# A chunked linear-attention recurrence and a two-layer MLP: the attention's instructions put in one planned order, the triangular inverse on blocks of 16, PSUM emptied by ScalarE in two places

## The chip, the cores and the metric

The kernel runs on one core of one Trainium2 chip. The metric is the device time of one execution in microseconds (us). Three runs of the kernel before took 845.59, 844.03 and 843.01 us; their median is 844.03 us.

## The reference

Six inputs of shape 4 x 8 x 768 x 40 (batch, heads, time, width) go through a recurrence with a 40 x 40 state per batch and head. The result, 3072 tokens of 320 values, goes through an MLP of 320 -> 2048 -> 320. The weights arrive in double precision.

```python
for t in range(S):
    y[:, :, t] = einsum('bhd,bhde->bhe', rt, state)
    Sa = einsum('bhde,bhe->bhd', state, at)
    state_decay = state * wt[:, :, None, :] - einsum('bhd,bhe->bhde', Sa, bt)
    state = state_decay + einsum('bhd,bhe->bhde', vt, kt)
...
h = x @ w_in
g = h * tanh(softplus(h))
return g @ w_out
```

## The kernel before

**Chunks.** The 768 time steps are cut into 12 chunks of 64. The 32 pairs of batch and head lie on two halves of the partitions (al), two groups (be) and eight slots. Inside a chunk the recurrence is turned into matrix products; between chunks only the state is carried. All attention work is fp32, where one matmul leaves two records in the profile (a transpose one).

**Preparation** (`pre_a`, once for each chunk and each be, 24 in all) loads decays and inputs (wa, bk), runs a forward and a backward scan over the decays on VectorE (lines 147, 157), scales a, b and k with them (152, 170), and has ScalarE copy the scaled a into ad (155). TensorE multiplies ad with bk (186, tile pa); ScalarE and VectorE take the results out of PSUM into GP (188, 189), HA (190) and, masked, HA (191). TensorE transposes bk (202) and ScalarE copies it to bkn (203). The backward scan writes into the place where a lay, so it waits for ScalarE's copy of a.

**Inverse** (`pre_inv` and `post_inv`, once for two chunks, six in all): 128 triangular 32 x 32 matrices lie across the partitions as lanes. VectorE transposes them in (209), then eliminates 30 rows one after another, each with a product into tmp (214) and an addition into XL (216), and transposes them out (218, 220). TensorE joins two 32-blocks to a 64-block with 32-wide products (232, 241); ScalarE lays the pieces out in bdT (249 to 251); TensorE forms the key products from bdT and HA (258), and ScalarE copies them to KT (260).

**Step** (`step_a` to `step_c`, once for each chunk, 12 in all, for two groups g): ScalarE copies the state ST into VS (277); TensorE multiplies VS with KT (284, tile pu); ScalarE negates the result into UVT (286). Then come products with r (314, tile pq, masked by VectorE into UVQ in 316), transposes of UVT (293) and of the state (304), and the products for the output y and the new state (334, 339). VectorE adds the new state from PSUM (342) and scales it (346); ScalarE copies y (343). GpSimd's queue stores y and the scan P to DRAM and loads the next chunk's r and v. "Double step" below means two chunks: one inverse, four preparations, two steps.

**MLP.** `load_x` reads y and P of a chunk back, multiplies them (565) and splits the product into a high and a low part (566 to 568). `mlp1` makes four first-layer groups (583, tile ph), `mlp2` the second layer (603 to 605, tile po), three groups later. The weights are turned from double precision into a high and a low single-precision part by `split`: a DMA into cv_d, then ScalarE (459), three VectorE operations (461 to 463), ScalarE (494) and VectorE (495). One such job covers 512 columns of w_in or 640 of w_out. Three jobs run early, nine for w_in late in the attention (`first`), three for w_out behind them (`second`), five in the MLP (`third`). They use one buffer each up to the MLP, and `first` may start only once all preparations have given back their memory.

**What sets the order.** The scheduler of the tile layer orders each engine's instructions. It is steered by priorities: a table OFF of offsets for each kind of work, ORDER and SORD for the sequence in which the source names it. It works on single instructions, so matmuls of two pieces of work may alternate on TensorE.

## Time and profile before

| | |
|---|---|
| median of three runs | 844.03 us |
| profiled execution, first to last instruction (the only time that its page gives) | 843.5 us |
| instructions in the profile | 18796 |
| TensorE matmul busy / VectorE / ScalarE / GpSimd | 89% / 55% / 51% / 12% |
| chain that ended last, by engine | PE 62%, DVE 15%, ACT 15%, issue 5%, DMA 2% |
| HBM traffic | 48.79 MB read, 11.86 MB written, 72 GB/s over the span |

PE is TensorE's matmuls, PEld its weight loads, DVE VectorE, ACT ScalarE, POOL GpSimd, SP the engine that issues most DMAs. Busy times of matmuls include a modelled end, so neighbouring matmuls overlap in the listing: the rate of a block is read from the start of its first matmul to the start of the next block. PEclk is the clock granted to TensorE, as a share of full speed. A share over the whole span mixes the attention with the MLP, which keep different engines busy.

### The profile page before, as it was taken

To read this page: it belongs to the slowest core of one execution; us is meant where nothing else is said; L and a number is where in the kernel's file an instruction comes from. 1 tells how busy PE (TensorE), PEld (TensorE's weight loads), DVE (VectorE), ACT (ScalarE), POOL (GpSimd) and SP (SyncE) were. 2 spreads that over 40 slices of the span, in tenths; PEclk is the share of its full clock that TensorE was granted. 3 is DMA by queue.
4 is the path that set the end of the run, shared out by engine and by line. 5 is a ranking of instruction groups with operands and counts; after the bars stand their busy time and mean duration, and the time that the engine had idled before them with its cause. 6 is when DMAs were issued, how large, how long until landed. Compare 5 with 4: busy or idle time off the path is not lost.

```text
span 843.5 us, 18796 instructions
## 1 busy us (share of the span) xinstructions
PE 748.6 (89%) x7816; PEld 695.6 (82%) x7816; DVE 462.0 (55%) x975; ACT 429.0 (51%) x937; POOL 103.3 (12%) x182
## 2 busy tenths in 40 slices
PE   2645898998989889889799899999999999999998
PEld 2534697887868778778768799999999999999998
DVE  6789879739899658788924639221222222122110
ACT  4533647774586866566738546333333333333331
POOL 8100012113122023221101200000000000000000
PEclk9855689899999999899959999999999999999999
DMA  6422223323423233323425734211120111100000
GB/s 177 134 71 64 74 63 73 90 67 105 129 81 80 66 88 103 82 67 96 123 66 142 179 109 128 54 35 36 38 54 25 31 54 35 35 21 16 16 1 32
DMA packets 58212, 61.91 MB, mean 73 GB/s; under 512 B 25536, under 2 KB 48704, under 8 KB 58128
## 3 DMA queue, kind: packets, MB, share of 16 engines
q1 hardware_dynamic: 49296, 40.94, 17.6%
q0 software_dynamic: 8832, 19.79, 9.5%
q8 instruction: 61, 1.00, 0.5%
q14 instruction: 23, 0.19, 0.1%
HBM read 48.79 MB, written 11.86 MB: 72 GB/s over the span
## 4 chain that ended last, share of the span: by engine, by line
PE 62%; DVE 15%; ACT 15%; issue 5%; DMA 2%; ACTq 0%; DVEq 0%; SPq 0%
PE ph L583 21%; PE po L604 7%; PE po L605 7%; PE po L603 7%; PE pa L186 5%; PE pa L258 4%; PE pq L314 3%; PE pq L334 2%; DVE XL L216 2%; DVE tmp L214 2%; ACT ad L155 2%; PE pu L284 1%; DMA cv_d<-in_wo 1%; DVE P L147 1%; ACT bdT L250 1%
## 5 line engine op out<-in xcount | busy, mean ns | idle before, releaser
L583 PE MATMUL ph<-xh,w_ih 128*128 128x256 f32 x576 | 148.3, 283 | 0.5 <-ACT xh L566 0.5
L585 ACT ACTIVATE g<-ph 128x512 f32<-128x512 f32 x96 | 57.3, 598 | 179.3 <-PE ph L583 179.2
L589 DVE TENSOR_TENSOR gl<-g,gh 128x1024 fp32r<-128x1024 f32 x48 | 58.7, 1225 | 160.7 <-ACT gh L588 160.4
L583 PE MATMUL ph<-xh,w_il 128*128 128x256 f32 x576 | 123.6, 283 | 0.0
L186 PE MATMUL pa<-bk,ad 128*128 128x168 f32 x384 | 85.0, 373 | 42.7 <-DVE bk L170 15.0
L604 PE MATMUL po<-w_ol,gh 128*128 128x320 f32 x384 | 118.8, 310 | 0.1
L605 PE MATMUL po<-w_oh,gl 128*128 128x320 f32 x384 | 118.4, 309 | 0.0
L603 PE MATMUL po<-w_oh,gh 128*128 128x320 f32 x384 | 117.7, 309 | 0.0
L186 PEld LDWEIGHTS pa<-bk,ad 128*128 128x128 f32 x384 | 70.8, 233 | 47.8 <-issue 22.8
L583 PEld LDWEIGHTS ph<-xh,w_ih 128*128 128x128 f32 x576 | 109.3, 190 | 0.7 <-ACT xh L566 0.7
L583 PE MATMUL ph<-xl,w_ih 128*128 128x256 f32 x384 | 101.2, 285 | 0.0
L583 PEld LDWEIGHTS ph<-xh,w_il 128*128 128x128 f32 x576 | 96.3, 190 | 0.0
L583 PEld LDWEIGHTS ph<-xl,w_ih 128*128 128x128 f32 x384 | 73.1, 190 | 0.8 <-issue 0.5
L604 PEld LDWEIGHTS po<-w_ol,gh 128*128 128x128 f32 x384 | 72.1, 188 | 0.5 <-DVE w_ol L495 0.5
L605 PEld LDWEIGHTS po<-w_oh,gl 128*128 128x128 f32 x384 | 72.1, 188 | 0.1
L603 PEld LDWEIGHTS po<-w_oh,gh 128*128 128x128 f32 x384 | 71.8, 188 | 0.0
L258 PE MATMUL pa<-bdT,HA 128*104 128x128 f32 x384 | 57.0, 304 | 9.0 <-ACT bdT L251 7.3
L258 PEld LDWEIGHTS pa<-bdT,HA 128*104 128x104 f32 x384 | 49.9, 190 | 14.4 <-ACT bdT L251 9.1
L216 DVE TENSOR_TENSOR XL<-XL,tmp 128x30 f32<-128x30 f32 (+9 forms) x180 | 59.0, 328 | 2.4
L214 DVE TENSOR_TENSOR tmp<-XL 128x30 f32<-128x30 f32 (+9 forms) x180 | 58.5, 325 | 2.5
L314 PE MATMUL pq<-bdr,UVT 128*128 128x128 f32 x384 | 57.3, 294 | 2.3 <-DVE UVQ L316 1.5
L314 PEld LDWEIGHTS pq<-bdr,UVT 128*128 128x128 f32 x384 | 50.8, 205 | 4.0 <-DVE UVQ L316 1.9
(89 smaller groups left out, 1243.5 us busy)
## 6 DMA issues: line engine op xcount, KB each, us to landing
wa<-in_wa SPq DMA_DIRECT2D x48, 162.5 KB
bk<-in_bk SPq DMA_DIRECT2D x48, 160.0 KB
cv_d<-in_wi SPq DMA_DIRECT2D x12, 512.0 KB
cv_d<-in_wo SPq DMA_DIRECT2D x8, 640.0 KB
pD<-P POOLq DMA_DIRECT2D x48, 81.2 KB, 2.2
VS<-in_vN POOLq DMA_DIRECT2D x24, 160.0 KB, 3.6
UVT<-in_vD POOLq DMA_DIRECT2D x24, 160.0 KB, 3.9
bdr<-in_rD POOLq DMA_DIRECT2D x24, 160.0 KB, 4.4
```

Of the source, the lines that this page charges most:

```text
L155: A.copy(ad[q, :, :, al], a[q].rearrange("p (s k t) -> p s k t", k=2, t=32))
L186: PE.matmul(pt[:, j], ad[:, s0 + j].rearrange("p k a t -> p (k a t)"), bk[:, s0 + j], start=(j == 0), stop=True, skip_group_check=True)
L214: V.tensor_tensor(out=tv, in0=X[:, i + 1:32, i:i + 1].broadcast_to([128, 31 - i, i]), in1=X[:, i:i + 1, 0:i].broadcast_to([128, 31 - i, i] ...
L216: V.tensor_tensor(out=X[:, i + 1:32, 0:i], in0=X[:, i + 1:32, 0:i], in1=tv, op=ALU.add)
L258: PE.matmul(pk[:, j], ha[:, s0 + j], bd[:, s0 + j].rearrange("p a t -> p (a t)"), start=(j == 0), stop=True, skip_group_check=True)
L314: PE.matmul(pq[:, s], UVT[:, g * 4 + s, be * 128:be * 128 + 128], br[:, be, g * 4 + s].rearrange("p a t -> p (a t)"), start=(s == 0), stop ...
L583: PE.matmul(o, w, x, start=(j == 0 and n == 0), stop=(n == 7), skip_group_check=True)
L585: A.activation(g[:, f0:f0 + 2], ph, AF.Mish)
L589: V.tensor_tensor(out=gl, in0=g, in1=gh.bitcast(F32), op=ALU.subtract)
L603: PE.matmul(po[k], gh[:, j, t], oh, start=(f == 0), stop=False, skip_group_check=True)
L604: PE.matmul(po[k], gh[:, j, t], ol, start=False, stop=False, skip_group_check=True)
L605: PE.matmul(po[k], gl[:, j, t], oh, start=False, stop=(f == 15), skip_group_check=True)
```

## The change

**One order for the attention.** All attention work and the conversions up to the MLP are recorded as operations in a small planner (`Plan`): engine, a cost in us written in the source, what is read and written, which buffers are used. `order` then runs a list: it takes the engine that can start earliest, and on it, of the operations that can start within 0.05 us of that, the one with the longest chain of costs behind it; a change of tile shape on TensorE counts 0.13 us, the scaling of the state has 15 us added to its chain. The operations are issued in the order of their planned starts, and this order stands as it is. An operation on TensorE is a whole block of matmuls. The MLP proper is still ordered by the tile layer, behind it. OFF, ORDER and SORD go.

**The inverse** eliminates rows inside 16 x 16 blocks only, both diagonal blocks in one instruction (14 pairs of row updates for 30). The block below the diagonal comes from two further products on TensorE, 128 matmuls of 32 x 32 x 16 each (lines 357 and 362 of the new kernel), with a ScalarE copy between them and a VectorE addition behind them. There is one more transpose, of half the size, into TD.

**PSUM.** In preparation ScalarE copies all of HA (104 columns for 40), and VectorE masks it afterwards in SBUF, once for eight slots. For y, ScalarE copies the new state's part out of PSUM too (524), and VectorE adds once for eight slots (528). To make HA one piece, k and b change places in the input layout.

**Buffers.** The backward scan has a tile E of its own. Two tiles of four PSUM banks each serve the attention, stn and the late conversions have two buffers, r and bdT one. `first` converts six jobs of w_in, `second` the last three of w_in and three of w_out; `second` starts only when `first` has finished.

```diff
-SORD = 'a0 b0 u0 d0 a1 b1 u1 d1 c0 c1'
-
-
-def at(tc, k):
-    return tc.high_priority(offset=OFF[k]) if OFF.get(k) else nullcontext()
...
+    def order(self):
+        for o in reversed(self.ops):
+            o.tail = o.cost + o.lat + max((p.tail for p in o.post), default=0.0) + o.late
...
+            e = min(low, key=low.get)
+            best = max((o for o in ready if o.eng == e and start[o] <= low[e] + self.look), key=lambda o: (o.tail, -o.i))
...
+        out.sort(key=lambda o: o.start)
+        return out
...
-        for i in range(1, 31):
-            tmp = iw.tile([128, 240], F32, name="tmp", bufs=NTMP)
-            tv = tmp[:, 0:(31 - i) * i].rearrange("p (t j) -> p t j", j=i)
...
+        op('V', 0.2, lambda: V.memset(X[:, 16:32, 0:16], 0.0), w=['X'])
+        x = X[:, 0:1, 0:1]
+        for i in range(1, 15):
+            m = 15 - i
...
+        op('V', 1.0, lambda: V.transpose(TD[:, :, 0:16].rearrange("p u j -> p j u"), X[:, :, 0:16].rearrange("p t j -> p j t")), r=['X'], w=['TD'])
...
+        def m1():
+            for u in range(32):
+                for q in (slice(k * 32, k * 32 + 32) for k in range(4)):
+                    PE.matmul(zv(b1)[q, u], gp.t[q, u, 1], TT[q, u, 16:32], start=(u == 0), stop=True, skip_group_check=True)
...
+                    PE.matmul(zv(b2)[q, u], TD[q, u], X1[q, u], start=(u == 0), stop=True, skip_group_check=True)
+        op('P', 3.0, m1, r=['TT'] + allg, w=[b1], mode=32)
+        op('A', 0.54, lambda: A.copy(X1, zv(b1)), r=[b1], w=['X'])
+        op('P', 3.0, m2, r=['TD', 'X'], w=[b2], mode=32)
+        op('V', 0.62, lambda: V.tensor_tensor(out=TT[:, :, 16:32], in0=TT[:, :, 16:32], in1=zv(b2), op=ALU.add), r=[b2], w=['TT'])
...
-            A.copy(ha[:, s0:s0 + m, oa:oa + 40], pt[:, 0:m, 128:168])
-            V.tensor_tensor(out=ha[:, s0:s0 + m, oh:oh + 64], in0=pt[:, 0:m, ok:ok + 64],
-                            in1=maskH.unsqueeze(1).broadcast_to([128, m, 64]), op=ALU.mult)
+            op('A', 0.38, lambda s0=s0, m=m, pv=pv: A.copy(ha.t[:, s0:s0 + m], pv()[:, 0:m, o2:o2 + 104]), r=[b], w=[(ha, s0)])
...
-                V.tensor_tensor(out=stn[:, 2 * s0:2 * s0 + 4], in0=st[:, 2 * s0:2 * s0 + 4, 0:40], in1=py[:, :, 64:104], op=ALU.add)
+                op('A', 0.25, lambda s0=s0, pv=pv: A.copy(stn.t[:, 2 * s0:2 * s0 + 4], pv()[:, :, 64:104]), r=[b], w=[(stn, s0)])
...
+            op('V', 0.42, lambda: V.tensor_tensor(out=stn.t, in0=stn.t, in1=st[:, :, 0:40], op=ALU.add), r=[('ST', g)], w=[(stn, 0), (stn, 2)])
...
+    M.first(S, S.after(preps, lambda: (pctx.close(), M.open_first(S))))
+    M.second(S, S.after(preps + invs + S.ops[-1:], lambda: (ictx.close(), M.open_second(S))))
+    with tc.manual_schedule():
+        S.issue()
```

Where the instructions stand now is shown at three places. Names are output<-inputs; the last column is the shape, x32 a count.

First TensorE, where an inverse's 32-wide products (232, 241) meet the products of a step's output (334), late in the program before:

```order
L232 MATMUL pa<-TT,GP 32x32 x32
L314 MATMUL pq<-bdr_121,UVT 128x128 x5
L241 MATMUL pa<-X_4875,GP 32x32 x20
L334 MATMUL pq<-UVQ_119,bkn 64x104
L241 MATMUL pa<-X_4875,GP 32x32
L334 MATMUL pq<-UVQ_120,bkn 64x104
```

The last rows go on alternating, one matmul of each. TensorE at an inverse of the new kernel, behind the output products of the step before (519 ends them; 289 is a small product of preparation, 357 and 362 the two new blocks, 474 the state's transposes, 327 transposes of preparation, 379 the former 232):

```order
L519 MATMUL pl_161<-bdr,smd_141 64x2x64 x4
L289 MATMUL pr_162<-w_98,cst 64x16 x2
L289 MATMUL pr_162<-w_99,cst 64x16 x2
L357 MATMUL pr_165<-TT,GP_151 32x16 x128
L474 MATMUL pl_160<-cst,ST_118 128x128 x4
L474 MATMUL pl_158<-cst,ST_119 128x128 x4
L362 MATMUL pr_164<-XL,TD 32x16 x128
L327 MATMUL pr_163<-cst,bk_90 128x128 x4
```

Blocks are whole now. Over the whole program TensorE changes between 32-, 64- and 128-wide tiles 243 times before and 120 times after.

Second VectorE at the start, around the opening transpose of the first inverse (209 before, 336 now; 147 and 266 are the forward scan, 170 and 277 the scaling of bk, 191 the mask of HA, 193 and 314 that of GP). Before:

```order
L191 TENSOR_TENSOR HA<-pa,cst 128x2x64
L193 TENSOR_TENSOR GP<-GP,cst 128x8x32
L146 RECIPROCAL d_102<-w_689 128x8
L209 STREAM_TRANSPOSE XL<-GP 128x32x32
L147 SCALAR_TENSOR_TENSOR P<-wa_96,d_102 128x520
L210 MEMSET XL 128x32
```

Now:

```order
L314 TENSOR_TENSOR GP_151<-GP_151,cst 128x8x32
L265 RECIPROCAL d_94<-w_99 128x8
L336 STREAM_TRANSPOSE XL<-GP_151 128x32x32
L266 SCALAR_TENSOR_TENSOR P_97<-wa_89,d_94 128x520
L337 MEMSET XL 128x32
L277 TENSOR_TENSOR bk_90<-bk_90,E 128x8x128
L338 MEMSET XL 128x16x16
L268 COPY w_99<-P_97 128x8
L344 TENSOR_TENSOR tmp<-XL 128x28
```

From there to the inverse's closing transpose, the order before holds nearly all of preparations five to eight between the row updates; the new one holds the three preparation rows shown and then row updates alone. Eight preparations precede the first step's product before, six now.

Third VectorE at the hand-over, ahead of the first x product of the MLP (565 before, 749 now). Before (461 to 463 and 495 are rows of a conversion, 316 masks of a step, 342 an addition to the state):

```order
L461 TENSOR_SCALAR cv_w<-cv_m 128x640
L462 SCALAR_TENSOR_TENSOR cv_w<-cv_m,cv_w 128x640
L463 SCALAR_TENSOR_TENSOR cv_w<-cv_d,cv_w 128x640
L316 TENSOR_TENSOR UVQ_119<-pq,cst 128x8x64
L495 SCALAR_TENSOR_TENSOR w_ol_5359<-cv_w,w_oh_5358 128x640
L316 TENSOR_TENSOR UVQ_120<-pq,cst 128x8x64
L565 TENSOR_TENSOR xy<-xy,xp 128x768
L342 TENSOR_TENSOR stn<-ST_122,pq 128x160
```

Now (661, 663, 665 and 668 are the same four rows of a conversion, of two jobs at a time):

```order
L668 SCALAR_TENSOR_TENSOR w_ol_6108<-cv_w,w_oh_6107 128x640
L668 SCALAR_TENSOR_TENSOR w_ol_6110<-cv_w,w_oh_6109 128x640
L661 TENSOR_SCALAR cv_w<-cv_d 128x640
L663 SCALAR_TENSOR_TENSOR cv_w<-cv_d,cv_w 128x640
L661 TENSOR_SCALAR cv_w<-cv_d 128x512
L665 SCALAR_TENSOR_TENSOR cv_w<-cv_d,cv_w 128x640
L663 SCALAR_TENSOR_TENSOR cv_w<-cv_d,cv_w 128x512
L665 SCALAR_TENSOR_TENSOR cv_w<-cv_d,cv_w 128x512
L668 SCALAR_TENSOR_TENSOR w_ol_6112<-cv_w,w_oh_6111 128x640
L668 SCALAR_TENSOR_TENSOR w_il_6106<-cv_w,w_ih_6105 128x512
L749 TENSOR_TENSOR xy<-xy,xp 128x768
```

Ten late conversions stand ahead of the first x product in both. Before, its neighbours belong to steps 10 and 11; now more than twenty rows of conversions lie between the last row of step 11 and it, and all ten jobs stand behind the last preparation. On TensorE the first MLP matmul stood ahead of the last y products of step 10 and now follows the last one of step 11.

More of the change, by code (lines that the diff above doesn't have):

```diff
@@ L110, in attention @@
         G.memset(b, 0.0)
[L111 removed]
+    for t in [d1] + [x.rearrange("p s k a t -> p (s k a t)") for x in adb]:
         A.copy(t, z.broadcast_to(t.shape))
[L113 to L118 removed]
@@ L119, in attention @@
-    ST = [cs.tile([128, 8, 64], F32, name=f"ST{g}") for g in range(2)]
-    for t in VS + [UVT] + bdr[:NBR] + ST:
-        G.memset(t, 0.0)
+    VS = tiles(cs, 2, [128, 2, 344], "VS")
+    UVT = cs.tile([128, 8, 256], F32, name="UVT")
+    UVQ = tiles(cs, 2, [128, 16, 104], "UVQ")
+    bdr = cs.tile([128, 2, 8, 2, 64], F32, name="bdr")
+    ST = tiles(cs, 2, [128, 8, 64], "ST")
+    newBKN = make(wk, NBKN, [128, 664], "bkn")
+    newKT = make(wk, NKT, [104, 8, 128], "KT")
+    newRW = make(wk, 4, [128, 2, 16], "rw")
@@ L123, in attention @@
+    newL = S.pool("psl", 4, [ps_l.tile([128, 512], F32, name=f"pl{i}") for i in range(4)])
+    newR4 = S.pool("psr", 4, [ps_r.tile([128, 512], F32, name=f"pr{i}") for i in range(4)])
+    for t in bdT + [TD] + [UVT, bdr] + VS + ST:
+        G.memset(t, 0.0)
+    for t in S.bkn:
+        G.memset(t[:, 640:664], 0.0)
+    op = S.op
+    view = lambda b, p, n, pat, **k: b.t[p, 0:n].rearrange(pat, **k)
+    full = slice(0, 128)
     RW, W2, HA, BKN, GP, KT = {}, {}, {}, {}, {}, {}
-    LQ, SQ, OQ, PQ = (dict(S=SP, G=G, A=A)[x] for x in QS)
@@ L300, in step_d, with tr @@
             return None
-        smd = wk.tile([128, 4, 128], F32, name="smd", bufs=2)
-        pt = ps_u.tile([128, 4, 128], F32, name="pu")
-        for s in range(4):
-            PE.transpose(pt[:, s], st[:, 2 * s:2 * s + 2].rearrange("p a d -> p (a d)"), ident)
-        A.copy(smd, pt)
+        smd, b = newSMD(), newL()
+        dv = lambda: view(b, full, 512, "p (s x) -> p s x", s=4)
+        def tr():
+            for s in range(4):
+                PE.transpose(dv()[:, s], st[:, 2 * s:2 * s + 2].rearrange("p a d -> p (a d)"), ident)
@@ L326, in step_c @@
         n = 64 if last else 104
+        bkns = [BKN[c, be] for be in range(2)]
         for s0 in range(0, 4, 2):
[L328 to L335 removed]
@@ new lines, in w_in, with w_out, cv @@
+    def w_in(self, wp, q):
+        self.ih.append(wp.tile([128, 3, 512], F32R, name=f"w_ih{q}"))
+        self.il.append(wp.tile([128, 3, 512], F32R, name=f"w_il{q}"))
+    def w_out(self, wp, q):
+        self.oh.append(wp.tile([128, 640], F32R, name=f"w_oh{q}"))
+        self.ol.append(wp.tile([128, 640], F32R, name=f"w_ol{q}"))
+    def cv(self, n, w, ctx=None):
+        p = self.tc.tile_pool(name=n, bufs=1, side="right")
+        p = ctx.enter_context(p) if ctx else self.cvx.enter_context(p)
+        return p.tile([128, w], F32, name="cv_w"), p.tile([128, w, 2], I32, name="cv_d")
@@ L533, in second, with first, open_second @@
+    def first(self, S, key):
+        new = S.pool("cva", 2)
+        ops = [self.plan_in(S, new, q, k, [key]) for q in (1, 2) for k in range(3)]
+        S.after(ops, lambda: self.cvx.close())
+    def open_second(self, S):
         self.ps_h = self.pool("ps_h", NH, space=PSUM)
-        if NQ1 < 4:
-            wp = self.wp = self.pool("w2b", 1)
-            with self.tc.tile_pool(name="cvb", bufs=CVB, side="right") as cv:
-                self.w_in(wp, cv, range(NQ1, 4))
         self.mpx = self.pool("mpx", 2)
@@ L539, in second @@
         self.mpa = self.pool("mpa", 2)
-        if NO1:
-            wp = self.pool("w2d", 1)
-            with self.tc.tile_pool(name="cvd", bufs=CVD, side="right") as cv:
-                self.w_out(wp, cv, range(NO1))
+        wp = self.pool("w2d", 1)
+        self.w_in(wp, 3)
+        for q in range(NO1):
+            self.w_out(wp, q)
+        self.cvx = ExitStack()
+        S.cvd[:] = [self.cv(f"cvd{i}", 640) for i in range(2)]
+    def second(self, S, key):
+        new = S.pool("cvd", 2)
+        ops = [self.plan_in(S, new, 3, k, [key]) for k in range(3)]
+        ops += [self.plan(S, new, lambda q=q: (self.oh[q], self.ol[q]), self.I['wo'][:, q * 640:(q + 1) * 640], [key], ('wo', q))
+               for q in range(NO1)]
+        S.after(ops, lambda: self.cvx.close())
```

640 lines of the change are left out of this document (376 added, 264 removed).

## The prediction

> **What bounds the kernel now.** First the page's totals, then the run cut into stages, then the rows at the cuts.
>
> ```profile
> PE 748.6 (89%) x7816; PEld 695.6 (82%) x7816; DVE 462.0 (55%) x975; ACT 429.0 (51%) x937; POOL 103.3 (12%) x182
> PEclk9855689899999999899959999999999999999999
> ```
>
> The totals name TensorE, but they average very different stages. The stage table (us from the start; busy time and instructions of each engine, then granted clock, DMA share, GB/s) is cut at the first matmul of step 0, at the first of step 10, and where MLP work fills PE.
>
> ```profile
> core 0: us, PE busy (x) PEld busy (x) DVE busy (x) ACT busy (x) POOL busy (x), PEclk, DMA share, GB/s
> 0.00:109.70 109.70, 60.16 (x375) 51.23 (x375) 90.42 (x207) 51.45 (x137) 25.64 (x48) 0.72 0.37 104
> 109.70:449.40 339.70, 302.36 (x4306) 263.34 (x4307) 254.93 (x631) 223.42 (x565) 68.42 (x120) 0.94 0.32 84
> 449.40:484.80 35.40, 31.12 (x385) 27.34 (x381) 21.09 (x36) 23.61 (x46) 8.30 (x12) 1.00 0.77 188
> 484.80:843.50 358.70, 354.95 (x2759) 353.71 (x2758) 95.59 (x102) 130.56 (x190) 1.00 (x2) 1.00 0.15 42
> ```
>
> The cuts, and two late pieces of the chain that ended last:
>
> ```profile
> 109.70 0.69 PE L284 MATMUL pu<-KT,VS 104*64 104x64 f32 x16
> 449.44 0.28 PE L284 MATMUL pu<-KT,VS 104*64 104x64 f32 x2
> 467.58 0.74 PE L583 MATMUL ph<-xh,w_ih 128*128 128x256 f32 x4 [0.47 <-ACT xh L566]
> ...
> 814.59 3.83 PE ph L583 x32
> 821.95 3.83 PE ph L583 x32
> ```
>
> Until 109.7 VectorE is the bound (90 of 110 us) and PE runs at clock 0.72. From there PE is busy 302 of 340 us. The MLP's beat is 821.95 - 814.59 = 7.36 us; 48 beats are 353.3 us. After the last first-layer block (ends 825.8) come four second-layer blocks of 3.52 us, to 839.9, and 3.6 us of copy and store. The MLP as it stands costs **357 us**, and the change leaves its inner loop alone. PE starts it at 467.6, mixed with steps 10 and 11; without the mixture it would have to start at 843.5 - 357 = 486.5. So the span is 109.7 (start) + 339.7 (ten steps) + 37.1 (to the MLP's effective start) + 357 = 843.5. I price the first three. The profiled execution's span is 843.5 us, 0.5 below the 844.03 median of the runs, so I add 0.5 at the end.
>
> **The change part by part.** *VectorE, inverse and preparation.*
>
> ```profile
> L216 DVE TENSOR_TENSOR XL<-XL,tmp 128x30 f32<-128x30 f32 (+9 forms) x180 | 59.0, 328 | 2.4
> L214 DVE TENSOR_TENSOR tmp<-XL 128x30 f32<-128x30 f32 (+9 forms) x180 | 58.5, 325 | 2.5
> ...
> L214 DVE TENSOR_TENSOR tmp<-XL 128x108 f32<-128x108 f32 x12 | 3.2, 267 | 0.2
> ...
> L152 DVE TENSOR_TENSOR wa<-wa,P 128x512 f32<-128x512 f32 x24 | 16.4, 685 | 0.0
> ...
> L209 DVE STREAM_TRANSPOSE XL<-GP x6: 2090/2124/2155, 49.9 to 375.2; 128x1024 f32<-128x1024 f32 x6
> ...
> 97.25 1.95 DVE TT L218
> ```
>
> Per double step 60 row updates (59.0 + 58.5 over 6 = 19.6 us) become 28, on 28 to 112 elements, 80 on the mean; at about 0.24 us (the 108-element row has 0.267) that is 6.7 us. Added are a half-size transpose (about 1 us, half of 2.1), an addition of 512 elements (0.69, as L152) and a small memset: **11 us less** per double step. The three masks of PSUM rows per preparation become one of 512 elements, and the state's two additions one, some 10 us less in the ten steps. In the ten steps VectorE's 254.9 us become about 254.9 - 5 x 11 - 10 = 190: it no longer comes near the bound.
>
> The start: the first inverse's opening transpose begins at 49.9 and its closing one at 97.25, because the order lays four more preparations between the row updates. Now only three preparation rows lie there. Ahead of the opening one stand two conversion rows instead of most of three jobs, but also part of a fifth preparation; I take it 5 us earlier, at 45. Then 2.1 + 6.7 + about 4 of rows between: the closing transpose at 58, **39 us earlier**. Behind it the path is longer: block, copy, block, addition, about 12 us at the clock of this stage (blocks priced below), then as before from 99.2 to 109.7. Step 0 starts at 58 + 2 + 12 + 10.5 = **82** (70 if the blocks run at full clock and nothing waits, 95 if preparations hold the path up).
>
> *TensorE.* The two new blocks are 128 matmuls of 32 by 32 by 16 each, 256 records since each fp32 matmul leaves two. The nearest rows are those of the inverse today, the second pair at a clock of 0.5:
>
> ```profile
> 279.50 0.24 PE L232 MATMUL pa<-TT,GP 32*32 32x32 f32 x2
> 279.68 0.55 PE L186 MATMUL pa<-bk,ad 128*128 128x168 f32 x2
> 280.16 0.24 PE L232 MATMUL pa<-TT,GP 32*32 32x32 f32 x2
> ...
> 283.27 1.20 PE L241 MATMUL pa<-X,GP 32*32 32x32 f32 x64
> 284.40 0.49 PE L314 MATMUL pq<-bdr,UVT 128*128 128x128 f32 x2
> ...
> 102.46 1.92 PE L241 MATMUL pa<-X,GP 32*32 32x32 f32 x64 [0.79 <-ACT X L235]
> 104.31 2.05 PE L186 MATMUL pa<-bk,ad 128*128 128x168 f32 x6
> 100.00:109.70 9.70, 8.91 (x129) 8.12 (x124) 9.46 (x25) 6.17 (x15) 1.01 (x2) 0.50 0.36 87
> ```
>
> 64 records take 284.40 - 283.27 = 1.13 us, 17.7 ns each; at half clock 1.85 us, 28.9 ns. The new ones stream half the columns and use four quadrants of the array, not two: between 8.8 (all halved) and 17.7 ns. I take 12, 3.1 us a block, between the ends and a little nearer the lower, since both changes point that way; both ends stay in the range. Five double steps in the stretch: 5 x 2 x 3.1 = **31 us more** PE (23 to 45).
>
> What PE loses: the alternation. In the rows above two records of each kind take 280.16 - 279.50 = 0.66 us, though L186's two need about 0.32 and L232's 0.035: about 0.15 us at each change of tile shape. The PE order has 243 such changes before and 120 now, about 105 fewer in this stretch: **-16 us**. It also makes up two preparations, since six and not eight now precede step 0: eight pairs like L186's (2.5 us) and eight transposes (about 0.9) each, **+7**. And stretches at half clock should go, which follow gaps:
>
> ```profile
> 346.00:348.00 2.00, 0.38 (x3) 0.38 (x4) 1.66 (x3) 1.52 (x5) 0.00 (x0) 1.00 0.62 181
> 350.00:352.00 2.00, 2.00 (x18) 1.55 (x18) 1.29 (x4) 1.04 (x3) 0.00 (x0) 0.50 0.00 0
> ```
>
> The clock of 0.94 over 339.7 us means 0.06 x 339.7 / 0.5 = 41 us at half speed, some 15 to 20 us lost; I expect 15 back. PE's busy time becomes 302 + 31 - 16 + 7 - 15 = 309. Against it stand 37 us of idle time before. Walking one double step through the new order by these durations, I find waits of about 1 us before the first block (closing transpose), 1.2 before the second (ScalarE copies four state slices first), 0.5 before the key products (ScalarE's lanes of bdT), 1 at the y products and 0.8 in preparation: 4.5, so 23 in all. The stretch becomes **332** (317 with nearly no waits, 361 if idle and half clock stay).
>
> *ScalarE.*
>
> ```profile
> L190 ACT COPY HA<-pa 128x120 f32<-128x120 f32 x48 | 12.4, 259 | 0.6
> L249 ACT COPY bdT<-TT 32x256 f32<-32x256 f32 x48 | 19.3, 403 | 3.5 <-DVE TT L218 2.6
> L260 ACT COPY KT<-pa 104x512 f32<-104x512 f32 x48 | 27.5, 585 | 18.3 <-PE pa L258 15.9 <-PE pu L284 1.6
> ```
>
> It takes over 44 copies of state (160 elements, about 0.29) = 13 us, larger HA copies (312 elements for 120, +0.16 x 48, and the small ones) = 10, six copies of 0.585 = 4; the bdT lanes, 72 of about 0.6 for 144 of about 0.4, give back 13. Net 14 us in the whole kernel on an engine that has 116 us free in the ten steps. It lies beside PE; were it uncovered it would cost those 14.
>
> *The hand-over.* Here the change loses time. In both orders ten late weight conversions stand ahead of the MLP's first x product on VectorE. Before, they began during step 8; now the first waits until the last preparation has freed its buffers, just ahead of step 10.
>
> ```profile
> 376.11 45.14 SPq L453 DMA_DIRECT2D cv_d<-in_wi  x7
> 434.85 13.84 SPq L453 DMA_DIRECT2D cv_d<-in_wi  x2
> ...
> 391.58 5.02 DMA cv_d<-in_wi
> 399.95 3.47 DMA cv_d<-in_wi
> ...
> 396.68 0.68 ACT L459 ACTIVATE cv_m<-cv_d 128x512 f32<-128x512 f32 x1 [2.09 <-DMA cv_d<-in_wi]
> 399.20 0.69 DVE L463 SCALAR_TENSOR_TENSOR cv_w<-cv_d,cv_w 128x512 int32<-128x512 int32 x1
> 400.75 0.69 DVE L495 SCALAR_TENSOR_TENSOR w_il<-cv_w,w_ih 128x512 fp32r<-128x512 f32 x1
> ```
>
> Nine loads were issued between 376.1 and 448.7, all ahead of step 10. A job is 3.5 to 5 us of DMA and 401.44 - 396.68 = 4.8 us of work. With two buffers five pairs follow one another: both loads about 5.5 (1 MB at the rates above), work of a pair 5 to 6, in all about 11. That is 55 us, counted from just ahead of step 10's first matmul; the first load overlaps the key products, x's own product, copy and difference add 3: the MLP starts about 58 us behind step 10, though PE, walked through the two steps and the last key products by the same durations, is done with step 11 after some 31. Then it starts cold, 2.5 us. **60.5 instead of 37.1** (40 if only VectorE's 26 us of conversions and its masks count, 70 if each pair also waits behind the steps' rows).
>
> *Sum.* 82 + 332 + 60.5 + 357 = 831.5 of span, 12 less than now; with the 0.5 to the median, **832**.
>
> **The rivals.** (a) *The feed is quicker.* If the pairs overlap fully, the hand-over takes 42: 813. For it: VectorE is busy only 21 of the 35 us after 449.4. Against: a job's buffer is freed only behind its third VectorE row.
> (b) *Slower: the clock drops in the small-tile stage.* In each double step PE runs the two blocks and four 32-wide products with waits between. A drop as at 348 to 355 (7 us) costs 3.5 us; two per double step are 35: 867. From 12 / 5 = 2.4 us per double step the gain is gone. For it, a window in which PE alternates 32-wide matmuls with y products:
>
> ```profile
> 424.00:426.00 2.00, 2.00 (x13) 1.16 (x11) 0.00 (x0) 0.00 (x0) 0.00 (x0) 0.50 0.00 0
> ```
>
> PE counts as busy there, and the clock is 0.50. Against: few such alternations remain, and blocks of 64 ran at full clock (283.27).
> The Trainium skill ("TensorE: Matmul & The Clock Gate", "What's actually happening") halves the clock after an idle window of about 3.4 us. The drop after 346 agrees, the one at 424 does not, and by the rule alone (b) would not occur.
> (c) *The order gains nothing.* A fixed queue that waits for the wrong thing keeps the old idle time and slow clock: 302 + 31 + 7 - 16 + 37 = 361, total 861. For it: the engines must keep to the durations that the order was made for. Against: VectorE and ScalarE have over 80 us idle each in the ten steps.
> (d) *A record has a fixed time.* If the 17.7 ns are no matter of columns and quadrants, a block costs 4.5 us: 10 x 1.4 = 14 more, 846. For it: halving the columns helps only if streaming sets those 17.7. Against: half the clock makes 28.9 of them, so part of it does.
> The Trainium skill ("TensorE: Matmul & The Clock Gate", "Wait — 56ns, not 53.3ns?") has such a floor: about 25 ns from start to start, however few the columns. By it a block would cost 6.4 us and the total come near 865; the 17.7 ns above lie under that floor, so (d) is priced by the row.
>
> **How the numbers follow.** Forecast 0.46 (817 to 846), (a) 0.13, (b) 0.15, (c) 0.15, (d) 0.11. The range 804 to 861 goes from a little under (a) to (c) and leaves out (b)'s upper half and the tails, about 2 in 10. About 0.3% (2.5 us) can be told from no change. Faster: most of the forecast (0.43), (a), a third of (d): 0.60. Same: 0.08, from (d) and the forecast's upper end. Slower: (b), (c) and what is left of (d), 0.32.
>
> **What would show it.** Step 0's first matmul near 82; step 10's near 414; a PE gap of 20 to 30 us between the last y product and the first ph, closed by a VectorE conversion; blocks of 256 records in 3.1 us; clock near 1.0 in the ten steps. It would be wrong if the blocks take over 4.5 us, if the clock falls to 0.5 in each double step, or if ph starts right behind step 11.

## The result, and the profile after

Slower, by 3.8%: 876.5 us (median of four runs, 871.7 to 881.9) against 844.8 for the kernel before on the same chip; ratio 1.038, 95% interval 1.032 to 1.045. The forecast was 832, with a range from 804 to 861. The profiled execution has a span of 880.1 us. Of the runs below, the profiled executions of spread_blocks and fill_small (843.0 and 923.4 us) lie at the slow end of their runs.

From the page of the changed kernel: busy time of each engine, the granted clock in 40 slices, and the queue that brings instructions.

```profile
PE 765.3 (87%) x10888; PEld 742.2 (84%) x10888; DVE 410.1 (47%) x731; ACT 433.9 (49%) x915; POOL 102.3 (12%) x166
...
PEclk9955995978699689859967959999999999999999
...
q8 instruction: 85, 1.39, 0.7%
```

VectorE lost 52 us of work and ScalarE gained 5. PE has 17 us more, and the clock now falls below 7 in five slices of the ten steps, where it did so once before. The stage table of the changed kernel, cut as before at the first matmul of step 0, of step 10, and of the MLP:

```profile
0.00:89.86 89.86, 47.28 (x832) 44.58 (x833) 60.25 (x119) 39.62 (x101) 23.99 (x44) 0.75 0.39 100
89.86:472.86 383.00, 333.89 (x6866) 315.54 (x6865) 217.25 (x449) 229.37 (x562) 71.77 (x112) 0.82 0.28 76
472.86:520.90 48.04, 28.34 (x505) 26.67 (x504) 33.37 (x55) 30.73 (x60) 6.53 (x10) 0.84 0.62 181
520.90:880.10 359.20, 355.80 (x2688) 355.46 (x2688) 99.25 (x110) 134.14 (x193) 0.00 (x0) 0.99 0.16 44
```

Against the working of the prediction (the MLP's 357 us are counted back from the end, as there):

| term | before | forecast | after |
|---|---|---|---|
| start, to step 0 | 109.7 | 82 | 89.9 |
| ten steps | 339.7 | 332 | 383.0 |
| hand-over (with the MLP's cold start) | 37.1 | 60.5 | 50.2 |
| MLP | 357 | 357 | 357 |

The loss is in the ten steps, and there it has two parts. The first shows in the groups of the two new blocks in that stretch (count, busy us and mean ns, idle time ahead and what ended it):

```profile
L362 PE MATMUL pr<-XL,TD 32*32 32x16 f32 x1280 | 20.1, 210 | 12.0 <-issue 12.0
L357 PE MATMUL pr<-TT,GP 32*32 32x16 f32 x1280 | 13.1, 181 | 12.6 <-issue 12.6
```

Ten blocks take 33.2 us of PE and another 24.6 in which PE stood still *inside* them, waiting for nothing that the profile shows: 5.8 us a block, not 3.1. Where the pauses lie is seen in PE's listing of the changed kernel (start, length, count, idle time ahead):

```profile
207.89 2.05 PE L357 MATMUL pr<-TT,GP 32*32 32x16 f32 x219
212.97 0.72 PE L357 MATMUL pr<-TT,GP 32*32 32x16 f32 x37 [3.03 <-issue]
...
286.17 1.16 PE L357 MATMUL pr<-TT,GP 32*32 32x16 f32 x116
287.55 1.26 PE L357 MATMUL pr<-TT,GP 32*32 32x16 f32 x128 [0.23 <-issue]
291.83 0.40 PE L357 MATMUL pr<-TT,GP 32*32 32x16 f32 x12 [3.02 <-issue]
...
449.13 0.61 PE L362 MATMUL pr<-XL,TD 32*32 32x16 f32 x28
451.08 1.91 PE L362 MATMUL pr<-XL,TD 32*32 32x16 f32 x128 [1.33 <-issue]
454.81 1.57 PE L362 MATMUL pr<-XL,TD 32*32 32x16 f32 x100 [1.83 <-issue]
```

At full clock a record takes 2.05 / 219 = 9.4 ns, less than the 12 I had put, and at half clock, as in the row at 451.08, 1.91 / 128 = 14.9. Both are a little high: a length holds the modelled end of its last record, some 0.2 us, and without it they are 8.5 and 13.3. Then PE stops, mostly for 1 to 3 us. Wherever one block has two pauses, exactly 128 records lie between them. The instruction queue says what 128 is. Its row before:

```profile
q8 instruction: 61, 1.00, 0.5%
```

It brought 61 packets, and now 85 of 16.4 KB: 24 more. Twelve blocks of 256 records with a weight load each are 6144 instructions, 256 to a packet, so a packet is 128 records. The counts of the page agree: matmuls and weight loads are 2 x 7816 before and 2 x 10888 now, 61.06 and 85.06 times 256. Where PE has run dry, packets are 291.83 - 287.55 = 4.3 and 454.81 - 451.08 = 3.7 us apart (3.5 to 4.3 over the five such blocks), about 30 ns a record, while the block eats one in 9 at full clock and one in 13 to 15 at half. The trace's DMA records show the cause itself: each of the 17 pauses ends 1.0 to 1.5 us after an instruction packet of 16 KB has landed, for instance at 211.51 for 212.97, at 290.41 for 291.83 and at 453.44 for 454.81.

The Trainium skill ("Runtime: NRT & Kernel Launch", "Instruction fetch mechanics") says that instructions come in blocks of 256, which agrees with the 128 records, and that the fetch is mostly hidden; for these blocks it was not.

The second part is the clock. Busy time and granted clock around one inverse of the changed kernel (the number ahead of the DMA share is the clock):

```profile
208.00:211.00 3.00, 1.94 (x219) 1.85 (x218) 3.00 (x9) 1.33 (x5) 2.78 (x4) 1.00 0.38 79
211.00:214.00 3.00, 1.03 (x39) 0.99 (x39) 2.90 (x7) 1.24 (x4) 1.03 (x2) 0.70 0.56 159
...
229.00:232.00 3.00, 3.00 (x99) 2.94 (x96) 1.94 (x5) 2.10 (x5) 0.00 (x0) 0.50 0.42 123
232.00:235.00 3.00, 3.00 (x16) 3.00 (x15) 2.26 (x2) 1.60 (x4) 0.00 (x0) 0.50 0.33 103
235.00:238.00 3.00, 3.00 (x40) 2.86 (x39) 2.90 (x8) 1.76 (x3) 1.02 (x2) 0.81 0.21 56
```

The clock halves in the first block's pause and stays at half for 24 us, although PE is busy without a gap from 221 on. Windows of 1 us show the same after each of the five inverses: 134 to 154, 212 to 236, 291 to 315, 369 to 393, 448 to 472. A clock of 0.82 over 383 us means 0.18 x 383 / 0.5 = 138 us at half speed, against 41 before.

### The profile page after: what moved, and what is told of

Its sections match the earlier page's. It is cut to its first block, busy times and chain, and to the rows that moved or that the text cites. A ratio compares the mean times of both kernels' runs of the same rounds, so it can differ in the third digit from the quotient of the medians.

```text
span 880.1 us, 24654 instructions
## 1 busy us (share of the span) xinstructions
PE 765.3 (87%) x10888; PEld 742.2 (84%) x10888; DVE 410.1 (47%) x731; ACT 433.9 (49%) x915; POOL 102.3 (12%) x166
## 4 chain that ended last, share of the span: by engine, by line
PE 78%; ACT 5%; issue 5%; DMA 4%; DVE 4%; SPq 0%; DVEq 0%; ACTq 0%
PE ph L767 21%; PE po L788 6%; PE po L789 6%; PE po L787 6%; PE pr L410 6%; PE pr L306 5%; PE pl L486 4%; PE pl L514 3%; PE pr L362 3%; PE pr L327 3%; PE pr L379 2%; PE pl L446 2%; DMA cv_d<-in_wi 2%; PE pl L459 2%; PE pr L357 2%
## 5 line engine op out<-in xcount | busy, mean ns | idle before, releaser
L767 PE MATMUL ph<-xh,w_ih 128*128 128x256 f32 x576 | 149.6, 285 | 18.5 <-ACT xh L750 18.5
L306 PE MATMUL pr<-bk,ad 128*128 128x168 f32 x384 | 81.1, 375 | 51.4 <-DVE bk L277 29.1
L306 PEld LDWEIGHTS pr<-bk,ad 128*128 128x128 f32 x384 | 72.9, 240 | 55.1 <-issue 15.3
L410 PE MATMUL pr<-bdT,HA 128*104 128x128 f32 x384 | 58.3, 325 | 1.3 <-ACT bdT L399 1.3
L410 PEld LDWEIGHTS pr<-bdT,HA 128*104 128x104 f32 x384 | 56.9, 215 | 1.9 <-ACT bdT L399 1.7
L277 DVE TENSOR_TENSOR bk<-bk,E 128x1024 f32<-128x1024 f32 x24 | 29.2, 1215 | 54.7 <-DMA bk<-in_bk 50.2
L772 ACT CAST gh<-g 128x1024 fp32r<-128x1024 f32 x48 | 50.3, 1048 | 1.2
L486 PE MATMUL pl<-bdr,UVT 128*128 128x128 f32 x384 | 46.0, 278 | 0.8 <-ACT UVT L449 0.8
L486 PEld LDWEIGHTS pl<-bdr,UVT 128*128 128x128 f32 x384 | 43.8, 192 | 1.7 <-ACT UVT L449 1.0
## 6 DMA issues: line engine op xcount, KB each, us to landing
pD<-P POOLq DMA_DIRECT2D x48, 81.2 KB, 2.3
```

The lines of the kernel that those rows point to most:

```text
L277: op('V', 1.14, lambda: V.tensor_tensor(out=bk4, in0=bk4, in1=E3[:, :, 0:64].unsqueeze(2).broadcast_to([128, 8, 2, 64]), op=ALU.mult), r=[ ...
L306: PE.matmul(pv()[:, j], ad[:, s0 + j].rearrange("p k a t -> p (k a t)"), bk[:, s0 + j], start=(j == 0), stop=True, skip_group_check=True)
L410: PE.matmul(kv()[:, j], ha.t[:, s0 + j], bd[:, o + s0 + j].rearrange("p a t -> p (a t)"), start=(j == 0), stop=True, skip_group_check=True)
L486: PE.matmul(qv()[:, s], UVT[:, g * 4 + s, 128 - be * 128:256 - be * 128], bdr[:, be, g * 4 + s].rearrange("p a t -> p (a t)"), start=(s == ...
L767: PE.matmul(o, w, x, start=(j == 0 and n == 0), stop=(n == 7), skip_group_check=True)
L772: A.copy(gh, g)
```

## The experiments

**The theories.** F: the blocks eat instructions faster than they come, and PE runs dry. T: 32-wide tiles do not count as work for the clock, so a block lowers it, pauses or not, and the 32-wide products behind it keep it low. Rivals: P, only pauses lower the clock; R, each small record simply costs some 20 ns and the pauses are part of that; O, the fixed order waits for the wrong things; V, VectorE.

All runs. Ratios are to the kernel before on the same chip; the stages are those of the profiled execution, and "pauses" those ended by issue in the two blocks, in the whole program.

| run | median us | ratio, 95% interval | step 0 | ten steps | clock there | pauses us | hand-over |
|---|---|---|---|---|---|---|---|
| before | 844.8 | | 109.7 | 339.7 | 0.94 | none | 34.9 |
| changed | 876.5 | 1.038 (1.032 to 1.045) | 89.9 | 383.0 | 0.82 | 29.0 | 48.0 |
| quarter_blocks | 829.0 | 0.990 (0.987 to 0.994) | 81.2 | 338.7 | 0.88 | 0 | 48.5 |
| old_inverse | 862.6 | 1.032 (1.026 to 1.037) | 85.9 | 382.4 | 0.83 | no blocks | 33.3 |
| burst_old_inverse | 931.3 | 1.112 (1.105 to 1.120) | 96.2 | 433.9 | 0.81 | no blocks | 33.1 |
| spread_blocks | 838.8 | 1.000 (0.995 to 1.004) | 95.9 | 355.0 | 0.87 | 5.7 | 32.9 |
| fill_wide | 885.0 | 1.052 (1.046 to 1.059) | 99.3 | 374.3 | 0.98 | 0.6 | 48.0 |
| fill_small | 915.9 | 1.085 (1.078 to 1.091) | 98.9 | 418.1 | 0.79 | 4.6 | 47.2 |
| fill_all | 903.8 | 1.070 (1.064 to 1.078) | 104.2 | 388.9 | 0.99 | 0.6 | 47.9 |
| true_costs | 854.9 | 1.016 (1.010 to 1.023) | 85.6 | 372.3 | 0.87 | 23.1 | 33.5 |
| before_blocks | 940.9 | 1.124 (1.113 to 1.134) | 94.1 | 441.4 | 0.84 | 17.5 | 42.7 |
| undo_empty | 875.0 | 1.043 (1.034 to 1.052) | 87.8 | 379.2 | 0.84 | 28.0 | 46.5 |
| combo4 | 818.3 | 0.979 (0.972 to 0.985) | 94.5 | 328.1 | 0.92 | 3.8 | 33.6 |
| combo8 | 836.4 | 0.997 (0.992 to 1.001) | 94.7 | 344.9 | 0.91 | 3.1 | 33.9 |

(The hand-over here runs to 359.2 us before the end.)

**quarter_blocks.** Fewer records in the same order; three quarters of the two blocks' products are left out:

```diff
-            for u in range(32):
+            for u in range(0, 32, 4):
```

> The two new blocks of each inverse issue 64 records instead of 256 (lane group u = 0, 4, 8, ... only; the products of the other 24 of 32 are left out, so the inverse's lower left 16x16 parts are not computed there). The order of every engine stays as in the changed kernel. Theory F (instruction supply: PE runs out of instructions inside a block, the pauses of 2 to 3 us ended by 'issue', and the half clock after them follows from these pauses): no issue pauses left inside L357 and L362, clock in the ten steps 0.95 or more, so 383 - 25 (pauses) - 45 (half clock) - 19 (three quarters of the block's own time) = about 295 to 305 for the ten steps; total 780 to 800. Rival R (each small record simply costs about 20 ns, pauses are part of it, the clock has another cause): three quarters of 5.5 us on 12 blocks = 50 us less, clock still near 0.82: about 830. Rival O (the fixed order waits for the wrong things): 860 or more.

No pause is left, and 44 of the ten steps' 383 us go; R, which allowed 50 us in the whole program, is hard to tell from that by time alone (829 against its 830). But the total for F, 780 to 800, was missed: I had laid all of the half clock at the pauses' door. Its ten steps:

```profile
81.17:419.82 338.65, 299.07 (x4946) 282.05 (x4945) 216.49 (x449) 228.38 (x563) 71.90 (x112) 0.88 0.32 85
```

Without one pause the clock is 0.88, below the 0.94 of before. So something else lowers it as well.

**old_inverse.** All 60 row updates on VectorE, no blocks, planned order.

```diff
-            m = 15 - i
-            tv = tmp[:, 0:2 * m * i].rearrange("p (b t j) -> p b t j", b=2, j=i)
...
-        op('P', 3.0, m1, r=['TT'] + allg, w=[b1], mode=32)
+        for i in range(1, 31):
+            m = 31 - i
+            tv = tmp[:, 0:m * i].rearrange("p (t j) -> p t j", j=i)
```

> The changed kernel with one part undone: the inverse eliminates all 32 rows on VectorE (60 row updates) and has no new blocks on TensorE; the planned order, ScalarE's emptying of PSUM and the hand-over stay. Theory F: no issue pauses, clock 0.93 or more in the ten steps, VectorE about 11 us per double step busier (270 of some 305 us); step 0 at about 84, ten steps 300 to 315, total 785 to 815, faster than the kernel before. Rival O (the order is at fault): 850 or more, clock below 0.9. Rival V (VectorE becomes the bound): ten steps 340 or more, PE waiting for VectorE, total 830 to 850.

F missed again; total and clock are those that O gave. What PE waited for in its ten steps (us, times, longest):

```profile
PE pr L358 <- DVE TT L345: 28.7, 4, 8.1
PE pr L305 <- DVE bk L276: 11.7, 6, 2.5
PE pr L358 <- DVE R L478: 8.6, 1, 8.6
```

PE is busy 303 of 382 us; four of its waits, of some 7 us each, are for the end of the row updates. So the reason is V's, with a larger price: in this order PE has too little to do beside some 20 us of row updates, and each long wait costs clock as well (beside each of the five longest, the clock is at 0.5 for 14 to 20 us). The blocks, slow as they are, cost the ten steps no more than what they replace (383.0 against 382.4).

**burst_old_inverse.** On top of it, one 32-wide product issued four times over:

```diff
-                for j in range(16):
+                for j in [*range(16)] * 4:
```

> old_inverse with one product of each inverse half (the 64 records of mx, 32x32 by 32 columns, 17.7 ns each at full clock) issued four times over in a row: 256 records in one burst, with no block of 16 columns anywhere; the result of the first pass is computed again. Plain cost 12 x 192 x 17.7 ns = 41 us. Theory F: a burst this fast also outruns the instruction supply: pauses ended by 'issue' inside it, 128 records apart when there are two, and half clock behind several of them; 60 to 100 us above old_inverse. Rival R (the pauses belong to the blocks of 16 columns on four quadrants): no issue pauses, clock as in old_inverse, 41 us above it or a little less.

69 us above old_inverse, within F's bounds, but not for F's reason: the longest pause in these bursts is 0.5 us. PE's listing and clock in one inverse, where two bursts stand back to back:

```profile
245.50 14.04 PE L358 MATMUL pr<-TT,GP 32*32 32x32 f32 x512 [8.14 <-DVE TT L345]
259.47 2.05 PE L305 MATMUL pr<-bk,ad 128*128 128x168 f32 x6
```

```profile
250.00:254.00 4.00, 4.00 (x159) 4.00 (x155) 3.20 (x7) 1.37 (x3) 1.03 (x2) 0.50 0.38 122
...
262.00:266.00 4.00, 4.00 (x62) 3.94 (x58) 0.00 (x0) 2.16 (x6) 0.00 (x0) 0.50 0.02 4
266.00:270.00 4.00, 3.81 (x34) 3.60 (x34) 3.10 (x7) 3.43 (x9) 0.57 (x2) 0.99 0.00 0
```

PE works for 14 us without a gap, and the clock does not rise; it rises 7 us later, behind a run of 128-wide matmuls. At half clock a record takes 14.04 / 512 = 27 ns, near the 30 at which instructions come, hence no pauses. This was the first sign of T: 32-wide work does not raise the clock.

**spread_blocks.** All records, in four chunks with other work between them:

```diff
-        op('P', 3.0, m1, r=['TT'] + allg, w=[b1], mode=32)
+        for u0 in (0, 8, 16, 24):
+            op('P', 0.75, lambda u0=u0: m1(u0), r=['TT'] + allg, w=[b1], mode=32, lat=0.15 if u0 == 24 else 1.6)
```

> The changed kernel with all 256 records of each block, issued in four chunks of 64; the planner is told that a chunk's successor may start only 1.6 us later, so it lays wider matmuls between them (the order of the rest is planned anew). Theory F: over 8 to 10 us the supply keeps up: issue pauses fall from 28 us in all to under 10, clock in the ten steps 0.90 or more, total 825 to 850. Rival R (the records themselves are slow): each chunk takes 1.3 us or more, clock near 0.82, total 875 to 890. Rival T (small tiles lower the clock, pauses or not): the pauses go but the clock stays near 0.82, total 850 to 870.

With as many small records, and planned anew, the pauses fall from 29.0 to 5.7 us, the ten steps by 28 and the total to that of the kernel before. R, which had 875 or more, falls. The clock, 0.87, stays below the 0.90 that F called for and above T's 0.82. The order also brought the hand-over down by 15 us, so not all of the 38 us belongs to the blocks.

**fill_wide and fill_small.** The pair that tells T from P: work *added* between the small records, in the same places and the same order, once on the whole array and once on one 32x32 tile.

```diff
+                if u % 4 == 3:
+                    PE.matmul(b1.t[:, 0:256], ident, z.broadcast_to([128, 256]), start=False, stop=True, skip_group_check=True)
```

> The changed kernel, same order on every engine, with work added: after every 32 records of the two new blocks one matmul of 128x128 by 256 columns whose moving operand is zero, so it adds nothing to the block's sums (8 per block, 16 per inverse; about 0.24 us a record, two records each, 3.8 us a block). The block's 256 small records are then spread over some 6 us. Theory F (instruction supply): no issue pauses in the blocks, since supply needs 128 records per 3.5 to 4 us. Theory T (32-wide tiles do not count as activity for the clock, so a block with its pauses lets the clock fall and the small products behind it keep it low; wide matmuls hold it up): clock in the ten steps 0.90 or more; although PE is given some 38 us more work there, ten steps take 345 to 365 and the total is 835 to 862, below the changed kernel's 876. Rival P (only the pauses lower the clock): the same here, but then fill_small does as well.

> As fill_wide, with the same number of added records of the same 256 columns at the same places, but on one 32x32 tile of the array instead of 128x128. Theory F: no issue pauses here either. Theory T: the clock falls all the same (0.83 or less in the ten steps), so the added work costs its 38 us and more at half clock: 885 to 915, 40 to 60 us above fill_wide. Rival P: clock and time as in fill_wide, within 10 us of it.

The ten steps of fill_wide:

```profile
99.26:473.51 374.25, 346.82 (x7025) 302.93 (x7024) 215.84 (x449) 227.26 (x562) 71.70 (x112) 0.98 0.29 78
```

and of fill_small:

```profile
98.89:517.02 418.13, 391.03 (x7025) 341.70 (x7025) 217.52 (x449) 229.47 (x562) 71.65 (x112) 0.79 0.25 69
```

The same number of records; 0.98 against 0.79 of the clock, and 44 us between them (31 by the medians, fewer than the 40 to 60 expected; fill_small's 915.9 lies at the edge of its 885 to 915). The mean clock of the whole execution tells them apart in every one of four runs each: 0.940 to 0.955 against 0.861 to 0.887. The wide zeros lift the clock from 0.82 to 0.98, and the ten steps are 9 us *shorter* with that work than without it. My total for fill_wide, 835 to 862, was too low: a filled block takes 8 us (215.5 to 223.4 in one case), not 6, so what the clock gave, the filler took, and step 0 comes 9.4 us later than in the changed kernel. That the pause is not needed for the drop is seen in fill_small around one block, which begins at 141.26 (busy time of PE, clock, DMA share, GB/s):

```profile
139.00:141.00 2.00, 2.00 (x48) 1.00 0.38 109
141.00:143.00 2.00, 2.00 (x114) 1.00 0.03 8
143.00:145.00 2.00, 1.64 (x81) 1.00 0.65 149
145.00:147.00 2.00, 2.00 (x78) 0.72 0.78 212
147.00:149.00 2.00, 2.00 (x32) 0.50 0.78 236
```

In these 10 us PE idles 0.36 us. The clock halves some 4.6 us after the small tiles begin. P falls.

**fill_all.** The same filler in the other 32-wide products too.

```diff
+                    if j % 8 == 7:
+                        PE.matmul(bx.t[:, 0:256], ident, z.broadcast_to([128, 256]), start=False, stop=True, skip_group_check=True)
```

> fill_wide, and the same zero matmuls after every 32 records of the inverse's other 32-wide products (mx and my, two more per product, 8 per inverse, about 3.8 us). Theory T: the stretch of 14 to 20 us behind each inverse that stays at half clock is gone, clock 0.93 or more in the ten steps; total within 10 us of fill_wide, on the lower side if what stays at half there is over 40 us. Rival: these products follow one another too quickly to matter: 19 us above fill_wide.

Clock 0.99, and 19 us above fill_wide: the rival. Once the blocks no longer lower the clock, single products of 64 records in between do not either; this filler bought nothing.

**true_costs.** Only numbers of the planner:

```diff
-        op('P', 3.0, m1, r=['TT'] + allg, w=[b1], mode=32)
+        op('P', 5.5, m1, r=['TT'] + allg, w=[b1], mode=32)
...
-            op('S', 0.1, lambda q=q, al=al: SP.dma_start(out=bk[q, :, xo:xo + 128], in_=I['bk'][c, be, al]), w=[('bk', be, al)], lat=2.5)
+            op('S', 0.8, lambda q=q, al=al: SP.dma_start(out=bk[q, :, xo:xo + 128], in_=I['bk'][c, be, al]), w=[('bk', be, al)], lat=4.0)
```

> The changed kernel with other numbers in its planner and nothing else: 5.5 us for each new block (3.0), and for the loads of wa and bk 0.4 and 0.8 us of issue and 4.0 us to landing (0.1, 0.1, 2.5), as the profile of the changed kernel has them. The order is planned anew. Theory O (the order was made for wrong durations): VectorE's 50 us of waiting for bk fall to under 25 and the total to 840 to 860. Rival (the loss is inside the blocks and in the clock): pauses and clock stay, total 865 to 885.

22 us less, with 23 us of pauses still there, and VectorE's waits for bk fall from 50.2 to 9.0: O is true beside F and T. Of the 30 us that its span is shorter, 11 lie in the ten steps and 14.5 in the hand-over, since the last preparation now ends early enough for the late conversions to begin at 421, 37 us ahead of step 10, and not at 465, 8 us ahead.

**before_blocks.** The new inverse alone, in the old scheduler:

```diff
-        for i in range(1, 31):
+        for i in range(1, 15):
...
+        for u in range(32):
+            for q in (slice(k * 32, k * 32 + 32) for k in range(4)):
+                PE.matmul(b1[q, u], gp[q, u, 1], TT[q, u, 16:32], start=(u == 0), stop=True, skip_group_check=True)
```

> One part of the change alone: the kernel before, with its own scheduler, and only the inverse replaced (28 row updates, half transpose, the two blocks of 128 matmuls, copy and addition). Theory F+T (blocks outrun the instruction supply and cost clock wherever they run in one piece): issue pauses inside the blocks, clock in the ten steps below 0.90, ten steps 345 to 375 against 340 before; the start gains 5 to 15 us from VectorE; total 840 to 870. Rival O (the fixed order alone is what cost the time): clock as before, total 820 to 835.

12% above the kernel before, far beyond both theories. The pauses (17.5 us) and the clock of the ten steps (0.84) are what F and T called for, but the total tests neither, for the old scheduler did not keep the blocks in one piece. PE's listing there:

```profile
215.16 0.49 PE L330 MATMUL pq<-bdr,UVT 128*128 128x128 f32 x2
215.58 0.23 PE L228 MATMUL pa<-TT,GP 32*32 32x16 f32 x2
215.74 0.49 PE L330 MATMUL pq<-bdr,UVT 128*128 128x128 f32 x2
216.16 0.23 PE L228 MATMUL pa<-TT,GP 32*32 32x16 f32 x2
```

Two small records with two wide ones take 0.58 us, where the small ones alone need 0.02. Counted over the traces, the ten steps hold 350 changes of tile shape here and 221 before; at the 0.15 us each of the prediction that is an estimate of 19 of the 102 us by which they are longer. How the rest divides was not measured. The new inverse was no gain without an order that keeps its blocks whole.

**undo_empty.** The state's additions back from PSUM by VectorE:

```diff
-                op('A', 0.25, lambda s0=s0, pv=pv: A.copy(stn.t[:, 2 * s0:2 * s0 + 4], pv()[:, :, 64:104]), r=[b], w=[(stn, s0)])
+                op('V', 0.29, lambda s0=s0, pv=pv: V.tensor_tensor(out=stn.t[:, 2 * s0:2 * s0 + 4], in0=pv()[:, :, 64:104], in1=st[:, 2 * s0:2 * s0 + 4, 0:40], op=ALU.add),
```

> The changed kernel with another part undone: the state products are again added from PSUM by VectorE (44 additions of 160 elements, about 0.29 us each) in place of ScalarE's 44 copies and 22 additions; the order is planned anew. If ScalarE's added work is covered, as the prediction had it: within 12 us of the changed kernel (865 to 890), pauses and clock as there. Rival (ScalarE's emptying is what makes PE wait): 10 to 25 us less and fewer waits of PE for ScalarE.

875.0, with the pauses as they were: this part of ScalarE's added work is covered. The HA copies and masks were not undone.

**combo4 and combo8.** spread_blocks and the loads' numbers of true_costs together; in combo8 eight chunks of 32 records, 0.9 us apart.

> The changed kernel with spread_blocks' four chunks of 64 records per block and true_costs' numbers for the loads together. Theories F and T with O: pauses under 10 us in all, clock 0.90 or more, hand-over near 33 us as in both, start near 86: total 815 to 835, faster than the kernel before. Rival (the two gains are the same time): 838 or more.

> As combo4 with eight chunks of 32 records and 0.9 us between them. Theory F: no pauses at all; about eight more changes of tile shape per block, some 1.2 us each block: total within 12 us of combo4, on either side. Theory T: clock 0.92 or more in the ten steps.

combo4 takes 818.3 us, 2.1% less than the kernel before (interval 1.5 to 2.8%) and 58 less than the changed one. Its first two stages:

```profile
0.00:94.50 94.50, 58.04 (x952) 53.91 (x952) 78.45 (x157) 50.83 (x131) 26.20 (x48) 0.80 0.45 120
94.50:422.56 328.06, 297.20 (x6751) 278.64 (x6745) 207.52 (x426) 221.73 (x540) 69.50 (x108) 0.92 0.32 87
```

The ten steps take 328, about the 332 that were forecast for the change, though at a clock of 0.92. combo8 has as few pauses and nearly the same clock, but PE is busy 309 us for 297 and the total lies 18 above: outside the 12 I allowed. Eight chunks make more changes of tile shape: counted over the traces, 196 in the ten steps against 132. At 0.15 us each that is an estimate of 10 us, most of what PE is busier; it was not tried apart.

## Why the prediction was wrong

**The step that failed: TensorE in the ten steps.** Of the 51 us by which they miss, 27 are the block. It was put at 3.1 us, from 64-record products, with bounds of 8.8 to 17.7 ns a record. At full clock the records kept to that (9.4 ns). But 64 records are half a packet of instructions and a block is two packets, so the rate of a short product was carried over to a block that outruns its supply; that rate of supply was in no row of before, because nothing there ran fast enough for long enough. The runs show 5.8 us a block, and the pauses all but gone when the same records are spread (spread_blocks) or filled up (fill_wide).

The other 24 us of the miss go with the clock. The prediction had "-15 half clock back"; instead the time at half rose from 41 to 138 us. Outside the blocks PE is busy 333.9 - 33.2 = 300.7 us, forecast 278: 23. fill_wide, with the same order at a clock of 0.98, gives the work alone: its ten filled blocks of some 8 us leave about 346.8 - 80 = 267 us of PE for the rest. By this estimate the half clock cost that work some 34 us, and the forecast had put the work itself some 11 too high, which hid part of the clock's cost.

The rest of the idle time, 49.1 - 24.6 = 24.5, is as forecast (23), but by luck. The walk had most of it at the blocks, the key products and the y products, and 0.8 us a double step, 4 in all, in preparation. Nearly all of it stands ahead of preparation's matmuls (306, 327), half of it for ScalarE's HA copies (us, times, longest):

```profile
PE pr L306 <- ACT HA L313: 12.3, 7, 2.5
PE pr L306 <- DVE bk L277: 6.5, 3, 3.6
```

So the order waits about as much as worked out, though elsewhere, and rival (c), as it was written, did not happen; true_costs shows that other numbers would still have given a better one.

**Rival (b) was half of the mechanism**, the clock, at 867, and was given 0.15. The other half, the supply, stood in no rival; (d) had a longer block, but from slower records. Two signs that the prediction named against itself came: blocks over 4.5 us, and half clock in each double step. The row that spoke for it, half clock in a window where PE alternated small tiles with y products, was the right one; I set against it that blocks of 64 ran at full clock. fill_wide, where the products of 64 have no filler and the clock is 0.98, agrees that these do no harm when they stand alone among wide work. Blocks of 256 do, and fill_small against fill_wide shows why.

The Trainium skill ("TensorE: Matmul & The Clock Gate", "What's actually happening") halves the clock after an idle window of about 3.4 us. fill_small speaks against idle alone: busy 9.64 of 10 us, and the clock fell. It agrees if 32-wide work is taken as idle. Nor does the drop after 346 in the kernel before bear the rule out, as the prediction had it: PE was idle there for 1.95 us and busy for the rest of the 3.5 us ahead of the drop. By the floor of 25 ns in the same page of the Trainium skill ("Wait — 56ns, not 53.3ns?") a block would take an estimated 6.4 us; 5.8 comes near that, but as bursts at 9.4 ns and pauses.

**The start.** The opening transpose came at 45.85, the closing one at 58.13, as forecast (45, 58). Step 0 came 7.9 us late:

```profile
64.62 0.94 PE L357 MATMUL pr<-TT,GP 32*32 32x16 f32 x54 [1.52 <-issue]
68.22 1.90 PE L362 MATMUL pr<-XL,TD 32*32 32x16 f32 x128 [0.77 <-issue]
72.22 0.94 PE L362 MATMUL pr<-XL,TD 32*32 32x16 f32 x55 [2.10 <-issue]
75.07 1.92 PE L379 MATMUL pr<-TT,GP 32*32 32x32 f32 x64
83.21 6.72 PE L410 MATMUL pr<-bdT,HA 128*104 128x128 f32 x32 [1.27 <-ACT bdT L399]
```

From the first block at 60.18 to the join (379) at 75.07 it is 14.9 us, forecast 12, and 4.4 us of pauses are among them. From there to step 0 at 89.86 it is 14.8, forecast 10.5, and 3.1 us of that difference are the key products: 32 records stand whole ahead of step 0 and take 6.65 us, where before 16 did, in 3.55 (106.15 to 109.70). Whole blocks cost here what the sum had carried over from the old order. quarter_blocks has step 0 at 81.2, as forecast, but there 384 of the 512 records are missing too, some 5 us at the 13.3 ns of half clock, so that agreement is luck.

**The hand-over** was the right mechanism, 10 us too long: the first late load was issued at 465.2, 7.7 us ahead of step 10 and not just ahead of it, and five pairs took 54 us to the last conversion's end at 519.1, 10.8 each for 11. PE idled 18.5 us there, forecast 20 to 30:

```profile
465.18 28.24 SPq L659 DMA_DIRECT2D cv_d<-in_wi  x6
```

```profile
518.45 0.69 DVE L668 SCALAR_TENSOR_TENSOR w_il<-cv_w,w_ih 128x512 fp32r<-128x512 f32 x1
519.06 0.95 DVE L749 TENSOR_TENSOR xy<-xy,xp 128x768 f32<-128x768 f32 x1
```

**VectorE and ScalarE** mattered little: VectorE is busy 217 us in the ten steps, 27 more than forecast (the sum added two preparations to PE's work and none to VectorE's), but never the bound, and ScalarE's copies of the state are covered, as undo_empty shows. For its HA copies that is not shown: PE's 12.3 us of waits for them are the largest item above, and no run gave them back to VectorE. The MLP is unchanged.

**What stays open.** How the clock's share of the loss, some 34 us by the estimate above, divides between blocks, pauses and the small products behind them was not measured apart. Nor was the exact share of small work at which the clock falls.

## What to carry to other kernels

Before work is moved to TensorE as many small matmuls, count its instructions against their supply, not only its columns against the array: here bursts of 256 records at 9.4 ns ran dry, while some 30 ns a record could be supplied. Look at the clock row, not only at the busy row: work on a small tile can be paid for by the wide work behind it. Both shrink when the burst is cut into pieces with wide work between them, which a planner does when it is told so: in combo4 the pauses fall from 29.0 to 3.8 us and the clock rises from 0.82 to 0.92.
